# A GEGLU feed-forward kernel: the order of the first loads and of the first matmuls

## The chip, the cores and the metric

The kernel runs on one core of a Trainium2 chip. Its time is the device time in microseconds (us); three runs of the kernel before gave 299.04, 299.29 and 299.55 us, so the median is 299.29 us. A further execution was taken with the profiler; all rows below come from it.

The engines are named as in the profile: PE is TensorE's matmul, PEld its weight load, DVE is VectorE, ACT is ScalarE, POOL is GpSimd and SP is SyncE, which only issues transfers here. "ps" is PSUM, where PE writes; it has eight banks.

## The reference

With x of 1024 tokens (32 x 32) by 1024, and weights 1024 x 3584, 1024 x 3584 and 3584 x 1024, all bfloat16:

```python
def reference(x, w_gate, w_up, w_down):
    return (_gelu(x @ w_gate) * (x @ w_up)) @ w_down
```

`_gelu` is the tanh approximation.

## The kernel before, in words

**Tiles.** A matmul here contracts over 128 rows. The model dimension of 1024 is cut into DK = 8 pieces, numbered dk; a weight piece is `big[w][:, dk, slot]`, 128 x 128, and x must lie transposed in `xT[:, dk, token]`. The 3584 hidden columns are FM = 28 chunks of 128. A "unit" (an entry of `parts`, and the p in the schedule) is one chunk with a range of tokens. Units 0 to 7 are chunks 0 to 7 with tokens 0 to 255 (XA); units 8 to 15 are the same chunks with tokens 256 to 511 (XB); the other units have 512 tokens. A unit has a gate sum ("G") and an up sum ("U") in PSUM; units 0 to 7 keep both in one bank, the bank of their own number. In the text, "gate step dk of unit p" is the matmul that adds piece dk to the gate sum of unit p.

**Transposing x.** The first 256 tokens come as two blocks of 128 tokens, `xa[:, 0]` and `xa[:, 1]`. PE turns pieces dk 0 to 4 of each block by a matmul against an identity (`turn_xa`, L349 to L360, ten turns of 128 columns), and ACT copies the turned pieces from PSUM to `xT` in four groups, `XA_PS` (L131), whose entries are (bank, first dk, last dk + 1, first block, last block + 1). DVE turns pieces dk 5 to 7 of both blocks (L457 to L466, 16 instructions, the mark "XD") and begins only when both blocks have landed. The other tokens come later and are turned by DVE (L476).

**The order of PE's work** is the list `steps`, written out by hand (L170 to L188). Ahead of it stand ten matmuls on constants that write nothing that is used (`WARM`, L395 and L399). Then, in this order: the turns of dk 0 to 2 of block 0 and of block 1, the turns of dk 3 and 4 of block 0 and of block 1; then step dk = 0 of units 0 to 7, G and U; then dk = 1 to 5 of these units with G and U by turns, and so on. Each step on units 0 to 7 waits for the pieces of `xT` that it reads, for its weight piece, and for the copy of a turned group that lay in its bank (L369 to L379). PE works strictly in the order of the list.

**The order of the loads.** SP issues block 0 of x, then the weight pieces dk = 0 to 7, gate and up by turns, 256 KB each (L293, `load_w0`); ACT issues block 1 of x on its own queue (L297). Both then wait for the up piece of dk = 5 to land, and issue the rest of x (L288). SP and POOL load the later weights when PE has finished with the buffers.

**After that** units 8 and up are worked one by one: ACT makes the gelu of a finished gate sum (L445), DVE multiplies it by the up sum (L485) into `hT`; at the end the down projection (L423) is summed over the 28 chunks, and ACT and DVE copy its results out.

## Time and profile before

| | |
|---|---|
| median of three runs | 299.29 us |
| profiled execution: time, and span of the core | 298.9 us, 297.6 us |
| PE busy | 293.7 us, 99% of the span |
| DVE, ACT, POOL busy | 64.3, 42.4, 7.9 us |
| first matmul on constants | 0.77 us |
| first turn (L355) | 3.93 us |
| first gate step (L386) | 5.01 us |
| DVE's 16 turns for XD | from 4.23 us, for 8.69 us |

A row of the timeline gives start, duration, engine, line, operation, tiles written and read, and "xN" for N instructions merged; in square brackets stands the idle time before, and what ended it. The table by stretch gives for each engine its busy time and the number of instructions that began. Matmuls are pipelined: one of 512 columns is shown as 379 ns long, but the next one follows 219 ns after it (49 in 10.74 us, on the chain). So a rate is read from the starts, not from the durations. Some records of matmuls are missing from the trace, at even distances.

### The profile page before, as it was taken

How to read it: one execution, taken by the hardware profiler on the slowest of the kernel's cores; microseconds unless marked ns; L12 is line 12 of the kernel's file. 1: busy time of each engine (PE TensorE's matmuls, PEld its weight loads, DVE VectorE, ACT ScalarE, POOL GpSimd, SP SyncE). 2: the span in 40 equal slices, each digit the busy share in tenths (PEclk: the TensorE clock that was granted, in tenths of full speed). 3: DMA queues.
4: the chain of work that ended last, by engine and by line, in shares of the span. 5: the costliest groups of instructions: out<-in, count | busy, mean ns of one | idle time of the engine just before them, and what ended most of it. 6: DMA issues, size and time to landing. Idle time of an engine off the chain costs nothing.

```text
span 297.6 us, 3492 instructions
## 1 busy us (share of the span) xinstructions
PE 293.7 (99%) x1528; PEld 148.3 (50%) x1552; DVE 64.3 (22%) x108; ACT 42.4 (14%) x79; POOL 7.9 (3%) x14
## 2 busy tenths in 40 slices
PE   8999999999999999999999999999999999999997
PEld 6899644444444444444444444444444444444445
DVE  4669721111221111122111122110000000000000
ACT  4032211211111121111121111110000000000000
POOL 1001001020000002001000000000000000000000
PEclk9999999999999999999999999999999999999999
DMA  7988004766009301943104000000000100010001
GB/s 260 389 199 266 19 2 149 274 204 222 0 0 303 122 0 40 373 153 99 45 0 141 0 2 0 0 0 20 18 18 18 37 18 18 20 35 18 18 20 35
DMA packets 17806, 26.43 MB, mean 89 GB/s; under 512 B 1152, under 2 KB 11392, under 8 KB 17792
## 3 DMA queue, kind: packets, MB, share of 16 engines
q1 hardware_dynamic: 13840, 16.78, 17.1%
q0 software_dynamic: 2176, 8.39, 7.9%
q10 hardware_dynamic: 1776, 1.05, 1.4%
q8 instruction: 12, 0.20, 0.3%
q14 instruction: 2, 0.02, 0.0%
HBM read 24.12 MB, written 2.10 MB: 88 GB/s over the span
## 4 chain that ended last, share of the span: by engine, by line
PE 99%; issue 0%; ACT 0%
PE ps L386 65%; PE ps L423 32%; PE ps L400 1%; PE ps L355 0%; ACT xT L451 0%
## 5 line engine op out<-in xcount | busy, mean ns | idle before, releaser
L423 PE MATMUL ps<-wd,hT 128*128 128x512 bf16 (+2 forms) x468 | 96.5, 366 | 0.4
L386 PE MATMUL ps<-xT,wubig 128*128 128x512 bf16 (+2 forms) x395 | 79.6, 336 | 0.3
L386 PE MATMUL ps<-xT,wgbig 128*128 128x512 bf16 (+2 forms) x394 | 79.3, 336 | 0.3
L423 PEld LDWEIGHTS ps<-wd,hT 128*128 128x128 bf16 x476 | 45.5, 98 | 51.6
L485 DVE TENSOR_TENSOR hT<-tb,ps 128x512 bf16<-128x512 f32 (+1 forms) x64 | 38.8, 611 | 136.2 <-PE ps L386 136.2
L445 ACT ACTIVATE tb<-ps 128x512 f32<-128x512 f32 (+1 forms) x64 | 34.3, 544 | 157.7 <-PE ps L386 157.5
L386 PEld LDWEIGHTS ps<-xT,wgbig 128*128 128x128 bf16 x400 | 38.2, 98 | 31.4 <-DVE xT L476 0.3
L386 PEld LDWEIGHTS ps<-xT,wubig 128*128 128x128 bf16 x400 | 38.2, 98 | 31.4
L386 PE MATMUL ps<-xT,wgsmall 128*128 128x512 bf16 x126 | 30.1, 379 | 0.1
L386 PE MATMUL ps<-xT,wusmall 128*128 128x512 bf16 x125 | 29.8, 379 | 0.2
L491 DVE CAST xT<-ps 128x512 bf16<-128x512 f32 (+1 forms) x8 | 5.4, 675 | 89.6 <-PE ps L423 89.6
L386 PEld LDWEIGHTS ps<-xT,wgsmall 128*128 128x128 bf16 x128 | 12.5, 98 | 15.1
L386 PEld LDWEIGHTS ps<-xT,wusmall 128*128 128x128 bf16 x128 | 12.5, 98 | 15.1
L451 ACT ACTIVATE xT<-ps 128x512 bf16<-128x512 f32 (+1 forms) x9 | 5.1, 561 | 93.1 <-PE ps L423 93.1
L476 DVE STREAM_TRANSPOSE xT<-hT 128x128 bf16<-128x128 bf16 (+2 forms) x20 | 13.4, 696 | 0.0
L461 DVE STREAM_TRANSPOSE xT<-hT 32x192 bf16<-32x192 bf16 x16 | 8.2, 514 | 4.7 <-DMA hT<-in_x_dram 4.2
L282 POOL DMA_DIRECT2D wubig<-in_w_up_dram x3 | 2.7, 884 | 63.1 <-PE ps L386 63.1
L400 PE MATMUL ps<-const-bfloat16-1.0 128*128 128x512 bf16 (+1 forms) x10 | 3.1, 498 | 0.8 <-PEq L528 0.8
L282 POOL DMA_DIRECT2D wusmall<-in_w_up_dram x2 | 2.0, 993 | 47.1 <-PE ps L386 26.0
L276 POOL DMA_DIRECT2D wd<-in_w_down_dram x3 | 2.3, 766 | 19.1 <-PE ps L386 19.1
L400 PEld LDWEIGHTS ps<-const-bfloat16-1.0 128*128 128x128 bf16 x10 | 1.2, 139 | 2.4 <-issue 2.4
L438 ACT ACTIVATE xT<-ps 128x128 bf16<-128x128 f32 (+1 forms) x4 | 1.6, 436 | 2.1 <-PE ps L355 2.0
(10 smaller groups left out, 4.9 us busy)
## 6 DMA issues: line engine op xcount, KB each, us to landing
wd<-in_w_down_dram SPq DMA_DIRECT2D x4, 1024.0 KB, 11.5
wgbig<-in_w_gate_dram SPq DMA_DIRECT2D x3, 1024.0 KB, 5.8
wubig<-in_w_up_dram POOLq DMA_DIRECT2D x3, 1024.0 KB, 9.7
wd<-in_w_down_dram POOLq DMA_DIRECT2D x3, 1024.0 KB, 11.3
wgbig<-in_w_gate_dram SPq DMA_DIRECT2D x8, 256.0 KB, 5.8
wubig<-in_w_up_dram SPq DMA_DIRECT2D x8, 256.0 KB, 5.9
wgsmall<-in_w_gate_dram SPq DMA_DIRECT2D x2, 1024.0 KB, 5.8
wusmall<-in_w_up_dram POOLq DMA_DIRECT2D x2, 1024.0 KB, 9.7
```

Of the source, the lines that this page charges most:

```text
L276: ew.do(lambda: eng.dma_start(wd[:, a:b, :], wd_r[:, a:b, :]), clock=clock)
L282: ctx.set((w, j), ew.do(lambda: eng.dma_start(wbuf(w, buf)[:, :, 0:gsz * P], w_r[w][:, :, c0 * P:(c0 + gsz) * P]), clock=q))
L386: v = pe.do(lambda: eng.matmul(ps[:, bank, f0:f1], wbuf(w, buf)[:, dk, slot * P:(slot + 1) * P], xT[:, dk, t0:t1], start=first, stop=last ...
L400: pe.do(lambda: eng.matmul(ps[:, 0, 0:n], ones_w, ones_x[:, 0:n], start=True, stop=True), mark=False)
L423: v = pe.do(lambda: eng.matmul(ps[:, b, 0:ncols], hT[:, m, tc * P:(tc + 1) * P], wd[:, m, col0:col0 + ncols], start=(m == 0), stop=(m == F ...
L438: ctx.set(("XA", j), act.do(lambda: eng.activation(xT[:, k0:k1, P * b0:P * b1], ps[:, bank, 0:nt * (k1 - k0)].rearrange("p (k t) -> p k t" ...
L445: ctx.set(("A", i), act.do(lambda: eng.activation(t_bufs[i % NTB][:, 0:t1 - t0], ps[:, gb, g0:g1], ACTF.Gelu_apprx_tanh)))
L451: ctx.set(("E", ji), act.do(lambda: eng.activation(osb[:, tc, col0:col0 + ncols], ps[:, b, 0:ncols], ACTF.Copy)))
L461: v = dve.do(lambda: eng.transpose(xT[32 * a:32 * (a + 1), XA_DVE[0]:XA_DVE[1], XA[0]:XA[1]].rearrange("p k (b t) -> p k b t", t=P)[:, :, ...
L476: v = dve.do(lambda: eng.transpose(xT[:, dk, q[0]:q[1]].rearrange("p (c i) -> p c i", i=32), src))
L485: ctx.set(("D", i), dve.do(lambda: eng.tensor_tensor(hT[:, m, t0:t1], t_bufs[i % NTB][:, 0:t1 - t0], ps[:, ub, u0:u1], ALU.mult)))
L491: ctx.set(("E", ji), dve.do(lambda: eng.tensor_copy(osb[:, tc, col0:col0 + ncols], ps[:, b, 0:ncols])))
```

## The change

Five edits that belong together:

- SP issues block 0 of x, then the gate piece of dk = 0, then block 1 of x, and then the other weight pieces in their old order. ACT issues no block.
- The ten turns go block by block: dk 0 to 4 of block 0, then dk 0 to 4 of block 1.
- After the turns of each block, five units (0, 1, 2, 6 and 3) do gate step 0 on the 128 tokens of this block alone. So these five steps become ten, of 128 columns instead of 256. The other steps with dk = 0 follow in a slightly different order.
- The four groups that ACT copies are cut by block: dk 0 of block 0, dk 1 to 4 of block 0, dk 0 of block 1, dk 1 to 4 of block 1. A step waits for a group only if it reads its tokens or uses its bank.
- `WARM` has one matmul of 128 columns at its end instead of four.

```diff
-    XA_PS = [(3, 0, 1, 0, 1), (7, 0, 1, 1, 2), (4, 1, 3, 0, 2), (5, 3, 5, 0, 2)]
+    XA_PS = [(3, 0, 1, 0, 1), (4, 1, 5, 0, 1), (5, 0, 1, 1, 2), (7, 1, 5, 1, 2)]
...
-    for k0, k1 in ((0, 3), (3, XA_DVE[0])):
-        for b in range(2):
-            steps += [("X", b, dk) for dk in range(k0, k1)]
-    for key, ps_ in (("G", (0, 1, 2, 6, 3, 7, 4)), ("U", (0, 1, 2, 3)), ("G", (5,)), ("U", (7, 6, 4, 5))):
+    FIRST = (0, 1, 2, 6, 3)
+    for b in range(2):
+        steps += [("X", b, dk) for dk in range(XA_DVE[0])]
+        steps += [(p, "G", 0, (P * b, P * b + P)) for p in FIRST]
+    for key, ps_ in (("G", (4, 5)), ("U", (0, 1, 2, 3)), ("G", (7,)), ("U", (6, 4, 5, 7))):
         steps += [(p, key, 0, None) for p in ps_]
...
+        def load_xa(ew, eng, b):
+            ctx.set(("xa", b), ew.do(lambda: eng.dma_start(
+                xa[:, b, :], xa_r[:, b, :]), clock=Q_XA[b]))
+
         def early_loads(ew, eng, side):
-            ctx.set(("xa", side), ew.do(lambda: eng.dma_start(
-                xa[:, side, :], xa_r[:, side, :]), clock=Q_XA[side]))
+            if side == 0:
+                load_xa(ew, eng, 0)
+                load_w0(ew, eng, "wg", 0)
+                load_xa(ew, eng, 1)
             yield
             if side == 0:
                 for k in range(DK):
                     for w in ("wg", "wu"):
-                        load_w0(ew, eng, w, k)
+                        if (w, k) != ("wg", 0):
+                            load_w0(ew, eng, w, k)
...
-            for jx, (xbank, k0, k1, _b0, _b1) in enumerate(XA_PS):
-                if t0 == XA[0] and (xbank == bank or k0 <= dk < k1):
+            lead = i < NBIG
+            for jx, (xbank, k0, k1, b0, b1) in enumerate(XA_PS):
+                if lead and (xbank == bank or (k0 <= dk < k1 and P * b0 < t1 and t0 < P * b1)):
                     pe.wait(C_ACT, ctx.get(("XA", jx)))
-            if t0 == XA[0] and dk >= XA_DVE[0]:
+            if lead and dk >= XA_DVE[0]:
                 pe.wait(C_DVE, ctx.get("XD"))
...
-        WARM = [512] * 6 + [128] * 4
+        WARM = [512] * 6 + [128]
```

## The prediction

> **What bounds the kernel now.** I read the chain that ended last first, since it says whether a saving at the start can reach the end at all. Its pieces are start, duration, what:

> ```profile
> PE 293.7 (99%) x1528; PEld 148.3 (50%) x1552; DVE 64.3 (22%) x108; ACT 42.4 (14%) x79; POOL 7.9 (3%) x14
> ```
> ```profile
> 0.77 3.14 PE ps L400 x10
> 3.93 1.26 PE ps L355 x10
> 5.19 28.03 PE ps L386 x288
> 33.22 0.05 issue
> 33.27 10.74 PE ps L386 x49
> ```

> PE works from 0.77 us to the end without a wait that shows; the pieces of 0.05 us "issue" recur every 10.79 us after 49 matmuls and are missing records. So whatever shifts PE's first step with dk = 1 shifts the end by as much, unless something else then binds. The whole case is the stretch up to there. The timeline of it:

> ```profile
> 0.73 0.38 SPq L297 DMA_DIRECT2D hT<-in_x_dram  x1
> 0.79 0.38 ACTq L297 DMA_DIRECT2D hT<-in_x_dram  x1
> ...
> 3.90 1.04 PEld L355 LDWEIGHTS ps<-ident,hT 128*128 128x128 bf16 x10 [0.26 <-issue]
> 3.93 1.26 PE L355 MATMUL ps<-ident,hT 128*128 128x128 bf16 x10
> ...
> 4.23 8.69 DVE L461 STREAM_TRANSPOSE xT<-hT 32x192 bf16<-32x192 bf16 x16 [4.23 <-DMA hT<-in_x_dram]
> 4.26 1.62 ACT L438 ACTIVATE xT<-ps 128x128 bf16<-128x128 f32 x4 [2.04 <-PE ps L355]
> ...
> 4.97 0.70 PEld L386 LDWEIGHTS ps<-xT,wgbig 128*128 128x128 bf16 x7
> 5.01 0.95 PE L386 MATMUL ps<-xT,wgbig 128*128 128x256 bf16 x7
> ...
> 6.78 1.04 PE L386 MATMUL ps<-xT,wgbig 128*128 128x256 bf16 x8
> ...
> 7.59 0.81 PEld L386 LDWEIGHTS ps<-xT,wubig 128*128 128x128 bf16 x8
> ```

> The turns begin at 3.93, the steps at 5.01, and the first step with dk = 1 at 6.78. Two rates lie in it. Until about 5 us PE runs at half speed: the last ten turns of 128 columns follow each other by (1.26 - 0.31) / 9 = 0.105 us, and the weight loads of the 512-column matmuls on constants start at 1.15, 1.57 and 2.00, 0.43 apart. Later 128 columns take 0.057 (four in 0.225 us at 19.89), 256 columns 0.109 (eight from 6.78 to 7.65), 512 columns 0.219. The column of the granted clock says 1.00 everywhere, so the starts have to be read.

> Then when the loads land. Block 0 of x lands 3.1 us after its issue (3.8), block 1 on ACT's queue 3.3 after (4.1), the gate piece dk 0 at 1.17 + 3.6 = 4.8, the up piece at 1.64 + 4.0 = 5.6, and those of dk 1 at 2.11 + 4.5 = 6.6 and 2.58 + 5.0 = 7.6. The stretch table (stretch, length, busy time of PE, PEld, DVE, ACT, POOL, granted clock, DMA share, GB/s):

> ```profile
> 1.00:2.00 1.00, 1.00 (x4) 0.29 (x2) 0.00 (x0) 1.00 (x1) 0.59 (x2) 1.00 0.17 51
> 2.00:3.00 1.00, 1.00 (x4) 0.44 (x3) 0.00 (x0) 0.21 (x2) 0.00 (x0) 1.00 0.96 264
> 3.00:4.00 1.00, 0.98 (x7) 0.46 (x6) 0.00 (x0) 0.00 (x0) 0.00 (x0) 1.00 1.04 387
> 4.00:5.00 1.00, 1.00 (x10) 0.96 (x11) 0.74 (x2) 0.69 (x3) 0.00 (x0) 1.00 1.14 397
> ```

> The 16 DMA engines are full from 2 us on. The issues stand 0.47 us apart and the landings 0.7 to 1.0, so bytes set the landings, not issues.

> **The loads, part by part.** A load's landing is when the bytes up to it have moved, and a lag. The two blocks are 524 KB; 51 + 264 = 315 KB had moved at 3.0, so 524 KB at 3.0 + 209/387 = 3.54, and the second had landed at 4.09: a lag of 0.55. In the new order, 262 KB (block 0 alone) have moved at 2.0 + 211/264 = 2.80, landing at 3.35; the gate piece comes at 3.54 + 0.55 = 4.09; block 1 is the third and comes at 4.0 + 84/397 + 0.55 = 4.76, where the gate piece was. So block 0 gains 0.45 us and the gate piece 0.7; block 1 loses 0.67. This is an estimate. Bounds: block 0 not sooner at all (3.8); or all sooner, so that loads do not bind. The up piece of dk 0 and the rest are issued one place, 0.47, later on SP's queue: nothing, since the bytes ahead of them stay the same. ACT's queue loses an issue of 0.38 us beside its 1.28 us table load; it then idles 2.04 us, so nothing.

> **PE, part by part.** Three matmuls on constants go: 3 x 0.107 = 0.32 us, so PE is free at 3.39 (3.28 + 0.107). It is worth something only if block 0 is there: from landing to first turn is 3.93 - 3.8 = 0.13.

> New on the path is the way from a block's first turn to the step that reads it. Today's row: the turn of dk 0 of block 1 is the fourth, at 3.93 + 3 x 0.105 = 4.25; ACT copies it from 4.58 for 0.28; the first step starts at 5.01. That is 0.76 us, and the other turns hide all but 0.03 of it. In the new order five turns of 0.107 = 0.53 stand between, so PE idles 0.76 - 0.53 = 0.23 us, and does so twice, once a block.

> The split steps: five of 128 columns at half speed cost 0.53, five at full speed 0.28, together 0.81 against 5 x 0.109 = 0.55. Then eleven steps of 256 columns, 1.20. Weight loads (98 ns, five more) lie beside the matmuls.

> The sum, if loads never bind: turns from 3.39, steps from 4.15 to 4.68, turns to 5.21, steps from 4.68 + 0.76 = 5.44 to 5.73, and 1.20 more: dk = 1 begins at 6.93 instead of 6.78, +0.15. By the bytes: turns from 3.35 + 0.13 = 3.48, steps from 4.24 to 4.77 (the gate piece is ready at 4.22), block 1 from 4.89, steps from 5.65 to 5.93, then 7.13, +0.35. With block 0 as late as now: turns from 3.93, steps from 4.69 to 5.2, block 1 from there, steps from 5.96 to 6.25, then 7.45, +0.67. I take +0.3, between the first two: the bytes are the nearest row, but the row of 264 GB/s holds the second queue's start too, which goes away.

> What else could bind: DVE starts its 16 turns when block 1 is there, 4.76 + 0.14 = 4.90 instead of 4.23, and is done 8.69 later, at 13.59 instead of 12.92. The first step with dk = 5 loads its weights at 13.65 now, and at 13.95 with the shift. So 0.36 us of cover remain; without it, DVE's lateness would be paid in full. ACT's larger copy (0.60, of dk 1 to 4 of block 0) ends near 4.8, before block 1's first turn needs ACT at 5.0. The pieces of dk 1 land at 6.6 and 7.6; the later PE asks for them from 7.1 and 7.95. So the cost of 0.3 stands, and beside the median of 299.29 gives 299.6. (The profiled execution took 298.9, its span 297.6 and 1.3 around it; it lies 0.39 under the median, and the shift is added to the median.) A change of under 0.2%, 0.6 us, cannot be told from none here.

> **Rival 1, slower: the half speed lasts longer.** Full speed came near 5.1 us, after 4.3 us of work with one idle of 0.22 (from 3.71 to 3.93). The new order has the idle of 0.23 at 3.92 and a second, equal one near 5.3, just where full speed began. If idles start the count anew, 4.3 us count from the first one's end (4.2) to 8.5, or from the last one's (5.6) to 9.9. From 5.6 on PE then does half the work it would: (8.5 - 5.6) / 2 = 1.45 or 2.15 us lost. With the smaller, 299.6 + 1.5 = 301.1. It decides if full speed comes after 6.3 or so. For it: the four times spread by 0.65 us, more than a fixed start would give, and what 1.3 us more of half speed would cost. Against it: the idle of 0.22 before did not prevent full speed.

> [...]

> **Rival 2, slower: block 0 lands no sooner.** Its first packets may simply be slow; only 51 GB/s show between 1 and 2 us, when block 0 is alone anyway. Then the trimmed matmuls on constants are replaced by waiting, and the sum is the third above: 299.29 + 0.67 = 299.96, 300.0. Against it: from 2.25 us or so the two blocks share full engines.

> **Rival 3, faster: late weights go away.** The up piece of dk 1 lands at 7.6 just as its first weight load starts (7.59). In other executions it may come later and stall PE; that could be the 0.39 of the median over the profiled one. Fewer queues at the start might bring all pieces sooner. That gives 299.29 - 0.39 + 0.15 = 299.05, and with full speed from 4.2 on (the first five steps then 0.25 shorter) 298.8; a little run-to-run luck makes it over 0.2%. Against it: DVE's chain, begun by block 1, allows no gain at all unless block 1 lands by 4.8.

> **How the numbers follow.** The sum as forecast (299.6, own range 299.2 to 299.9): 0.42. Rival 1 (301.1): 0.27. Rival 2 (300.0): 0.19. Rival 3 (298.8 to 299.05): 0.12, of which 0.08 over the bound. Faster 0.08, within 0.2% 0.42 + 0.04 = 0.46, slower 0.27 + 0.19 = 0.46. The range from 299.0 to 301.2 leaves out most of rival 3 and the upper part of rival 1, about 0.2.

> **What would show it.** First turn at 3.4 to 3.5 (rival 2: 3.9); two gaps of 0.2 us in PE's starts, behind the fifth and the tenth turn; DVE's turns from 4.6 to 4.9; the first dk = 1 step at 6.9 to 7.15; no wait at dk = 5. Starts of 256-column steps 0.21 apart after 6 us would show rival 1. The prediction is wrong if dk = 1 begins before 6.7, or if the steps are still at half speed at 7 us.

## The result, and the profile after

Over 17 runs each, the changed kernel takes 300.26 us in the median (299.45 to 301.81) and the kernel before 299.18 us (298.91 to 299.94). The ratio of the means is 1.0041, with a 95% interval from 1.0026 to 1.0057: slower by 0.41%, that is 1.1 us by the medians and 1.2 by the means. The time lies inside the range of the prediction (299.0 to 301.2), but beyond its likeliest case (299.6, no change that can be told).

The times of the changed kernel do not scatter around one value. Sorted:

```
before: 298.91 298.96 298.98 299.04 299.05 299.13 299.15 299.18 299.18 299.23 299.29 299.45 299.46 299.46 299.55 299.67 299.94
after:  299.45 299.48 299.67 299.88 299.90 299.94 300.06 300.12 300.26 300.28   300.68 301.00 301.38 301.39 301.60 301.76 301.81
```

Ten are 0.3 to 1.1 us over the old median, seven are 1.5 to 2.6 us over it. The profiled execution took 299.9 us, so it belongs to the ten. Its timeline (start, duration, engine, line, operation):

```profile
0.72 0.38 SPq L298 DMA_DIRECT2D hT<-in_x_dram  x1
...
1.17 0.42 SPq L294 DMA_DIRECT2D wgbig<-in_w_gate_dram  x1
...
1.63 0.42 SPq L298 DMA_DIRECT2D hT<-in_x_dram  x1
...
3.65 0.73 PE L363 MATMUL ps<-ident,hT 128*128 128x128 bf16 x5
...
4.53 0.71 PE L395 MATMUL ps<-xT,wgbig 128*128 128x128 bf16 x5 [0.16 <-DMA wgbig<-in_w_gate_dram]
...
5.17 0.75 PE L363 MATMUL ps<-ident,hT 128*128 128x128 bf16 x5
5.22 3.79 DVE L470 STREAM_TRANSPOSE xT<-hT 32x192 bf16<-32x192 bf16 x7 [5.22 <-DMA hT<-in_x_dram]
...
5.87 0.67 PE L395 MATMUL ps<-xT,wgbig 128*128 128x128 bf16 x7
...
7.41 1.04 PE L395 MATMUL ps<-xT,wgbig 128*128 128x256 bf16 x8
```

The turns of block 0 begin 0.28 us sooner than the first turn before (3.65 against 3.93), but block 1 is turned only from 5.17, and the first step with dk = 1 begins at 7.41 instead of 6.78: +0.63. The rest of the loss stands much later, among the waits of PE's weight loads:

```profile
6.42 0.33 PEld L395 LDWEIGHTS ps<-xT,wubig 128*128 128x128 bf16 x4 [0.16 <-DMA wubig<-in_w_up_dram]
...
17.71 0.10 PEld L395 LDWEIGHTS ps<-xT,wubig 128*128 128x128 bf16 x1 [0.49 <-DMA wubig<-in_w_up_dram]
```

The last up piece (dk = 7), issued at 9.38, landed 8.3 us later at 17.67. PE's starts have a hole there of 0.37 us beyond their usual distance. 0.63 + 0.37 = 1.00, and the two profiled executions differ by 299.9 - 298.9 = 1.0.

### The profile page after: what moved, and what is told of

It reads as the page before. It is cut to its first block, busy times and chain, and to the rows that moved or that the text cites. A ratio compares the mean times of both kernels' runs of the same rounds, so it can differ in the third digit from the quotient of the medians.

```text
span 298.6 us, 3520 instructions
## 1 busy us (share of the span) xinstructions
PE 295.6 (99%) x1554; PEld 147.9 (50%) x1554; DVE 64.4 (22%) x108; ACT 42.6 (14%) x79; POOL 7.9 (3%) x14
## 4 chain that ended last, share of the span: by engine, by line
PE 93%; DMA 3%; SPq 3%; issue 0%; ACT 0%
PE ps L395 61%; PE ps L432 32%; DMA wubig<-in_w_up_dram 3%; SPq L294 2%; SPq L298 0%; ACT xT L460 0%
## 5 line engine op out<-in xcount | busy, mean ns | idle before, releaser
L395 PE MATMUL ps<-xT,wgbig 128*128 128x512 bf16 (+2 forms) x405 | 80.4, 335 | 0.2 <-DMA wgbig<-in_w_gate_dram 0.2
```

The lines of the kernel that those rows point to most:

```text
L395: v = pe.do(lambda: eng.matmul(ps[:, bank, f0:f1], wbuf(w, buf)[:, dk, slot * P:(slot + 1) * P], xT[:, dk, t0:t1], start=first, stop=last ...
```

## The experiments

Three theories were told apart. A: idle time of PE in the first microseconds keeps it at half speed for longer in some executions. B: the new order of the loads brings data late. C: the way from a turn over ACT's copy to the step is now paid for twice. Each batch was timed beside its own runs of the kernel before, with medians of 299.31 us (e1 to e4), 299.40 (e5 to e8) and 299.43 (e9 to e12); what is said of "over before" goes against these. The three batches ran on three different chips. Each ratio is one of means, with its 95% interval.

**e1_short_const: the shorter run on constants alone**

```diff
 (the kernel before)
-        WARM = [512] * 6 + [128] * 4
+        WARM = [512] * 6 + [128]
```

> The kernel before, with one 128-column matmul on constants instead of four, nothing else changed. PE's idle ahead of block 0 grows from 0.22 to about 0.54 us; no load and no step moves. Theory A (idle time early on makes PE stay at half speed longer in some executions): the times spread over more than the 1 us of the kernel before, some executions come out above 300.0, the median rises by 0.3 us or more. Theory B (the loss is late loads) and theory C (the loss is the wait for ACT's copy, paid twice): median and spread as before, 299.2 within 0.15, none above 300.1.

Measured: 299.16 us (298.88 to 299.75, 12 runs), ratio 0.9994 (0.9984 to 1.0003). PE's starts show the longer idle, 0.60 us ahead of the first turn, and the steps from 5.06 at full speed (seven of 256 columns from 5.06 to 5.82, 0.109 each):

```profile
2.42 1.17 PE L400 MATMUL ps<-const-bfloat16-1.0 128*128 128x512 bf16 x3
3.98 1.14 PE L355 MATMUL ps<-ident,hT 128*128 128x128 bf16 x10 [0.39 <-DMA hT<-in_x_dram]
5.06 0.92 PE L386 MATMUL ps<-xT,wgbig 128*128 128x256 bf16 x7
```

So this part of the change costs nothing, and an idle of 0.6 us in that stretch did not hold full speed back. A, in the form "any more idle", fell here.

**e4_order_only and e3_loads_only: the two halves of the change**

e4 keeps the old loads (block 1 on ACT's queue) and has all the rest of the change; e3 is the kernel before with the new loads alone.

```diff
 (e4: the changed kernel)
-            if side == 0:
-                load_xa(ew, eng, 0)
-                load_w0(ew, eng, "wg", 0)
-                load_xa(ew, eng, 1)
+            ctx.set(("xa", side), ew.do(lambda: eng.dma_start(
+                xa[:, side, :], xa_r[:, side, :]), clock=Q_XA[side]))
...
-                        if (w, k) != ("wg", 0):
-                            load_w0(ew, eng, w, k)
+                        load_w0(ew, eng, w, k)
```
```diff
 (e3: the kernel before)
-            ctx.set(("xa", side), ew.do(lambda: eng.dma_start(
-                xa[:, side, :], xa_r[:, side, :]), clock=Q_XA[side]))
+            if side == 0:
+                load_xa(ew, eng, 0)
+                load_w0(ew, eng, "wg", 0)
+                load_xa(ew, eng, 1)
...
-                        load_w0(ew, eng, w, k)
+                        if (w, k) != ("wg", 0):
+                            load_w0(ew, eng, w, k)
```

> The changed kernel with the old loads (block 1 on ACT's queue, gate piece third). Turns, split steps, groups and the short run on constants as in the changed kernel. Block 0 lands at 3.8, so turns from 3.93; the gate piece at 4.8, so steps from 4.93. Theory C: dk = 1 begins 7.3 to 7.7, all weight pieces land as before, time about 299.9 to 300.1 with little spread. Theory B: under 299.5, the loads being the old ones. Theory A: the spread of the changed kernel, some above 301.

> The kernel before with the new order of loads alone (block 0, gate piece, block 1, all on SP). The turns of block 1 stand fourth in PE's list and wait for block 1 near 5.1, so about 1.2 us of idle. Theory B: dk = 1 begins near 7.7 (+1.0), all weight pieces land 0.4 us later than before, the up piece of dk 7 past 17 us again, time 300.2 to 300.6. Theory A adds executions with 1.5 us on top: up to 302. Theory C alone: under +0.5.

Measured: e4 300.86 us (299.32 to 301.58, 12 runs), ratio 1.0042 (1.0025 to 1.0059), with 7 of 12 over 300.6. e3 300.52 us (300.1 to 302.36, 7 runs), ratio 1.0057 (1.0034 to 1.0081). Each half is slower alone. e3's median is theory B's number, and three of its seven executions lie near 302, as A adds. Its profile is of one of these, 302.05 us. PE waits there for block 1 and then for the up piece of dk 0, and the granted clock is 0.50 from 7.42 to 10.83 us:

```profile
5.40 0.64 PE L362 MATMUL ps<-ident,hT 128*128 128x128 bf16 x7 [1.21 <-DMA hT<-in_x_dram]
...
7.30 0.96 PE L393 MATMUL ps<-xT,wubig 128*128 128x256 bf16 x4 [0.23 <-DMA wubig<-in_w_up_dram]
```

e4's spread is theory A's; both B (under 299.5) and C (299.9 to 300.1 with little spread) miss it. e4's profile is of an execution of 301.55 us:

```profile
2.85 0.74 PE L402 MATMUL ps<-const-bfloat16-1.0 128*128 128x512 bf16 x2
3.91 0.73 PE L356 MATMUL ps<-ident,hT 128*128 128x128 bf16 x5 [0.32 <-DMA hT<-in_x_dram]
5.00 0.72 PE L388 MATMUL ps<-xT,wgbig 128*128 128x128 bf16 x5 [0.36 <-DMA wgbig<-in_w_gate_dram]
5.51 0.74 PE L356 MATMUL ps<-ident,hT 128*128 128x128 bf16 x5
6.19 1.14 PE L388 MATMUL ps<-xT,wgbig 128*128 128x128 bf16 x7
7.12 1.06 PE L388 MATMUL ps<-xT,wubig 128*128 128x256 bf16 x4
7.98 0.42 PE L388 MATMUL ps<-xT,wgbig 128*128 128x256 bf16 x1
8.19 1.06 PE L388 MATMUL ps<-xT,wubig 128*128 128x256 bf16 x4
9.04 1.44 PE L388 MATMUL ps<-xT,wgbig 128*128 128x256 bf16 x8
```

Four 256-column steps take from 7.12 to 7.98, 0.21 each: half speed, until past 9 us. Ahead of it PE stood for 0.53 us (3.28 + 0.107 to 3.91), 0.57 (behind the fifth turn, to 5.00) and 0.15 (to 6.19): 1.25 us of idle in less than 3.

**e2_filled and e5_order_filled: the idles filled**

Both put 128-column matmuls on constants into the idles, and leave loads and useful steps alone: e2 in the changed kernel, e5 in e4. A step "W" is such a matmul, with its bank and, where that bank was being copied, the group to wait for.

```diff
 (e2: the changed kernel)
+        steps += [("W", 0, None)] * 3 if b == 0 else [("W", 4, 1)]
         steps += [(p, "G", 0, (P * b, P * b + P)) for p in FIRST]
+        if b == 0:
+            steps += [("W", 7, None)]
...
-        WARM = [512] * 6 + [128]
+        WARM = [512] * 6 + [128] * 3
...
```
```diff
 (e5: against e4)
+        steps += [("W", 0, None)] * 4 if b == 0 else [("W", 4, 1)]
...
-        WARM = [512] * 6 + [128]
+        WARM = [512] * 6 + [128] * 5
...
```

> The changed kernel with matmuls of 128 columns on constants put into PE's idles: two more ahead of block 0, three behind its turns, one behind its steps, one behind the turns of block 1. Loads and useful work as in the changed kernel. Theory A: the executions above 300.6 go away, the median falls from 300.3 to 299.7 to 299.9. Theories B and C: the idles are waits on loads and copies and stay as long, so median 300.2 to 300.3 and executions up to 301.8 as in the changed kernel.

> The new order of PE's work with the old loads (as e4), and matmuls of 128 columns on constants in the idles: four more ahead of block 0, four behind its turns, one behind the turns of block 1. No useful step moves. Theory A (a window of about 3.4 us with too much idle takes or withholds full speed): the executions above 300.6, 7 of 12 in e4, go away or fall to 1 in 10; median 299.7 to 300.0. Rival (those executions come from late weight pieces or from the wait for ACT's copy): 4 or more in 10 stay above 300.6, median 300.6 to 300.9.

Measured: e5 299.88 us (299.24 to 300.28, 12 runs), ratio 1.0012 (1.0002 to 1.0023): none of 12 over 300.6, against 7 of 12 in e4. That is theory A's number: of the 1.55 us that e4's median lay over before, about 1.1 go (0.9 by the means) when PE is merely kept busy. Its profile has three idles of 0.38, 0.35 and 0.23 us left there, and full speed from 3.43 us on (four 256-column steps from 6.32 to 6.76, 0.11 each), in spite of a wait of 0.87 us for the gate piece of dk 1 at 8.17:

```profile
4.35 0.39 PE L413 MATMUL ps<-const-bfloat16-1.0 128*128 128x128 bf16 x4
4.93 0.45 PE L389 MATMUL ps<-xT,wgbig 128*128 128x128 bf16 x5 [0.19 <-DMA wgbig<-in_w_gate_dram]
```

e2 gained little, and theory A's number is missed there: 300.14 us (299.91 to 302.25, 10 runs), ratio 1.0033 (1.0019 to 1.0047), 4 of 10 over 300.6. The profile of its 302.25 us says why, and shows the loss of full speed best of all. PE's timeline, then the table by stretch (stretch, length, busy time and count of PE, PEld, DVE, ACT, POOL, granted clock, DMA share, GB/s):

```profile
4.80 0.22 PE L422 MATMUL ps<-const-bfloat16-1.0 128*128 128x128 bf16 x1
6.35 0.53 PE L366 MATMUL ps<-ident,hT 128*128 128x128 bf16 x5 [1.32 <-DMA hT<-in_x_dram]
```
```profile
0.77:3.75 2.98, 2.98 (x11) 1.33 (x12) 0.00 (x0) 1.44 (x2) 0.76 (x2) 1.00 0.59 183
3.75:7.16 3.41, 1.81 (x24) 1.30 (x23) 0.73 (x2) 1.34 (x4) 0.00 (x0) 1.00 0.94 305
7.16:10.57 3.41, 3.41 (x20) 2.44 (x19) 3.22 (x7) 0.35 (x1) 0.00 (x0) 0.50 1.06 405
10.57:14.00 3.43, 3.43 (x34) 3.06 (x32) 3.21 (x7) 0.00 (x0) 0.00 (x0) 1.00 1.05 388
```

The 1.00 of the first row is not to be trusted: the turns of 128 columns start 0.107 us apart until 3.70, which is half speed. Full speed came at 3.75. Block 1 landed only at 6.3, one matmul on constants could not cover that, and PE was busy for 1.81 of the 3.41 us from 3.75 to 7.16. For the next 3.41 us the granted clock is 0.50, though PE is busy all the time; then it is 1.00 to the end. e3's record has the same steps at 4.00, 7.42 and 10.83. So in these two profiles the granted clock changed at borders 3.41 us apart, and half speed followed a stretch with long idles: up to 1.32 us in e2, up to 1.21 us in e3.

**e8_blockwise: block by block, without the split steps**

```diff
 (against e4)
         steps += [("X", b, dk) for dk in range(XA_DVE[0])]
-        steps += [(p, "G", 0, (P * b, P * b + P)) for p in FIRST]
-    for key, ps_ in (("G", (4, 5)), ("U", (0, 1, 2, 3)), ("G", (7,)), ("U", (6, 4, 5, 7))):
+    for key, ps_ in (("G", FIRST + (4, 5)), ("U", (0, 1, 2, 3)), ("G", (7,)), ("U", (6, 4, 5, 7))):
...
-        WARM = [512] * 6 + [128]
+        WARM = [512] * 6 + [128] * 4
```

> Old loads, four 128-column matmuls on constants, turns block by block and groups by block, but no split steps: all steps of dk 0 have 256 columns and come after the turns of both blocks. One idle is left, 0.76 - 0.53 = 0.23 us, behind the turns of block 1. Theory C: 299.3 to 299.6, that is 0.2 to 0.3 over before. Theory A: no executions above 300.6, since PE is busy for over 80% of every window. If instead turning block by block is what costs, 300 and more.

Measured: 299.55 us (299.2 to 301.2, 11 runs, one over 300.6), ratio 1.0002 (0.9988 to 1.0017). C has the right size at most: 0.15 over before, not told from nothing. A expected no execution above 300.6, and there is one, 301.2. Turning block by block does not cost that can be told; what e4 has on top is the split steps, with the waits ahead of and between them, and the shorter run on constants, which cost nothing by itself in e1. Those two were not tried apart in the new order.

**e7_one_queue and e10_one_queue_filled: the queue alone**

e7 is the kernel before with both blocks issued by SP (block 0, block 1, gate piece). e10 adds six matmuls of 128 columns on constants behind the turns.

```diff
 (e7: the kernel before)
-            ctx.set(("xa", side), ew.do(lambda: eng.dma_start(
-                xa[:, side, :], xa_r[:, side, :]), clock=Q_XA[side]))
+            if side == 0:
+                for b in range(2):
+                    ctx.set(("xa", b), ew.do(lambda: eng.dma_start(
+                        xa[:, b, :], xa_r[:, b, :]), clock=Q_XA[b]))
```
```diff
 (e10: against e7, behind the turns)
+    steps += [("W", 0, None)] * 6
...
```

> The kernel before with both blocks of x issued by SP, in the order block 0, block 1, gate piece, up piece; PE's order is the old one. If bytes alone set the landings (the prediction's step): block 0 lands near 3.4 instead of 3.8, block 1 and the weights as before, time 299.2 within 0.2. If one queue starts more slowly than two: the weight pieces of dk 1 and later land 0.3 to 0.5 later, and the time rises by 0.3 to 0.5.

> As e7 (the kernel before, both blocks and all weights on SP's queue), with six matmuls of 128 columns on constants behind the ten turns, 0.64 us at half speed, in the idle ahead of the gate piece. It parts the 1.1 us that e7 lost. Theory A has part of it: the idle is covered, the executions above 301 (4 of 12) go and the median falls to 299.8 to 300.1; what is left over 299.4 is the slower loading. If loads are all of it: median 300.5 as in e7.

Measured: e7 300.49 us (299.36 to 301.95, 12 runs), ratio 1.0043 (1.0026 to 1.006); e10 300.13 us (299.45 to 301.51, 12 runs), ratio 1.0025 (1.0012 to 1.0038). The blocks landed as early as by the bytes (3.4 and 4.0 us), but in e7's profile the gate piece behind them landed at 6.70, and PE waited for it:

```profile
3.70 1.23 PE L357 MATMUL ps<-ident,hT 128*128 128x128 bf16 x10
6.75 0.94 PE L388 MATMUL ps<-xT,wgbig 128*128 128x256 bf16 x7 [1.81 <-DMA wgbig<-in_w_gate_dram]
```

So with the old order of PE's work and the old order of loads, moving one 256 KB load to SP's queue cost 1.1 us (the weights behind it are issued 0.47 us later). Both of e7's expectations, 0 and 0.3 to 0.5, miss that. In e10 the median lies just above theory A's band and one execution, 301.51, is still over 301. The filler takes about a third of the cost back, though the two intervals overlap; that the 0.7 left is the waiting for data itself is argued, not shown.

The prediction's rule that bytes alone set the landings is refuted. By the packets in e7's trace, the 786 KB up to the gate piece had moved at 4.44 us. The trace also shows 16 signals for each of these loads, and PE's wait ended with the last of them: half of the gate piece's signals had come by 4.63, the last two at 6.06 and 6.70, and its first step began at 6.75. In the changed kernel's profile 15 signals of the last up piece had come by 16.63, the last came at 17.67, and the weight load that waited for it began at 17.71. In the kernel before all 16 for the gate piece came between 4.52 and 4.80.

**e9_act_block1: two queues, but the second one later**

```diff
 (the changed kernel)
                 load_w0(ew, eng, "wg", 0)
+            else:
                 load_xa(ew, eng, 1)
...
-            act.do(lambda: eng.activation(warm[:, 0:1], const0, ACTF.Gelu_apprx_tanh))
+            v = act.do(lambda: eng.activation(warm[:, 0:1], const0, ACTF.Gelu_apprx_tanh))
+            act.wait(C_ACT, v)
```

> The changed kernel, but block 1 is issued by ACT, behind its first activation (near 2.25 us), so that it still comes after block 0 and near the gate piece. PE's order and the matmuls on constants are those of the changed kernel. If it matters that two queues are at work at the start: 1.1 MB moved by 5 us instead of 1.0, the gate piece of dk 2 at about 8.2 instead of 8.65, the lower half of the times 0.3 to 0.5 under that of the changed kernel (its lowest is 299.45). If bytes alone set the landings: times as the changed kernel, median 300.3. Theory A in both cases: some executions above 300.6, since the idles stay.

Measured: 304.69 us (304.23 to 305.75, 4 runs), ratio 1.018 (1.016 to 1.0201): both expectations missed by far. Issued at 2.24 us behind SP's first weight pieces, block 1 landed at 8.25, and PE stood for it. Its steps then stay at half speed up to the first ones with dk = 1, at 11.85: 2.85 us from 9.00 on, where the profile of 299.9 us has 1.54 for the same steps (5.87 to 7.41):

```profile
4.46 0.71 PE L396 MATMUL ps<-xT,wgbig 128*128 128x128 bf16 x5 [0.19 <-DMA wgbig<-in_w_gate_dram]
8.30 0.76 PE L364 MATMUL ps<-ident,hT 128*128 128x128 bf16 x5 [3.12 <-DMA hT<-in_x_dram]
```

So a second queue at work did not make the loads quick by itself: 279 GB/s from 2 to 5 us. What the kernels with quick first loads (before, e1, e4, e5, e8: 334 to 358 GB/s) share is that both queues start in the first microsecond, with the two blocks ahead of any weights.

**e6_x_later: the rest of x issued one piece later**

```diff
 (the changed kernel)
-            ew.wait(Q_W0[("wu", 5)], ctx.get(("wu0", 5)))
+            ew.wait(Q_W0[("wu", 6)], ctx.get(("wu0", 6)))
```

> The changed kernel, but the rest of x is issued when the up piece of dk 6 has landed instead of that of dk 5, 1.3 us later. If the transfers of x delay the last weight pieces, the wait of 0.37 us before the up step of dk 7 goes and the lower half of the times falls by 0.2 to 0.4 (lowest 299.1 to 299.3 instead of 299.45). If x is then late for DVE's turns, PE waits after 19 us instead and the time is the same or longer. Theory A on its own: no change, median 300.3.

Measured: 301.3 us (299.82 to 303.31, 12 runs), ratio 1.0066 (1.0044 to 1.0088). The up piece of dk 7 landed 8.5 us after its issue at 9.19, again at 17.7, though x was issued from 15.21 on instead of 13.37: moving x's transfers back did not bring it sooner. Instead PE now waits for DVE near 20 us, as the other branch said:

```profile
20.20 0.34 PEld L395 LDWEIGHTS ps<-xT,wgbig 128*128 128x128 bf16 x2 [0.21 <-DVE xT L485]
```

That does not explain a median 1.9 us over before, against 1.1 for the changed kernel, with 10 of 12 over 300.6; in its profile block 1 was late before the edit can act (turns from 5.74). The two intervals overlap, and why so many executions fell there stays open.

**e11_after_look and e12_after_look2: the changed kernel twice more**

> The changed kernel once more, for a second profile of it. Theory A: if it takes over 300.6, starts of 256-column steps 0.21 apart are found for about 3.4 us after 5.5 us; if under 300.3, none after 6 us.

> The changed kernel a third time, for a third profile, with the same reading: over 300.6 with a stretch of half speed of about 3.4 us that ends past 8 us, or under 300.3 with none after 6 us.

Both were of the upper group: 301.5 and 301.78 us. PE's timeline of e12:

```profile
3.46 0.73 PE L363 MATMUL ps<-ident,hT 128*128 128x128 bf16 x5
4.22 0.69 PE L395 MATMUL ps<-xT,wgbig 128*128 128x128 bf16 x5
6.06 0.75 PE L363 MATMUL ps<-ident,hT 128*128 128x128 bf16 x5 [1.15 <-DMA hT<-in_x_dram]
6.75 1.14 PE L395 MATMUL ps<-xT,wgbig 128*128 128x128 bf16 x7
7.69 1.06 PE L395 MATMUL ps<-xT,wubig 128*128 128x256 bf16 x4
8.54 0.42 PE L395 MATMUL ps<-xT,wgbig 128*128 128x256 bf16 x1
8.76 1.06 PE L395 MATMUL ps<-xT,wubig 128*128 128x256 bf16 x4
9.61 1.08 PE L395 MATMUL ps<-xT,wgbig 128*128 128x256 bf16 x8
```

Block 1 comes at 6.0 instead of 5.1, PE idles for 1.36 us, and four 256-column steps take 0.85 us until past 9 us, as theory A expects: full speed comes at about 9.7 us (eight 256-column steps from 9.61 to 10.53, 0.115 each), in e11 at about 9.1. The first step with dk = 1 begins at 9.61 instead of 6.78: +2.83, and the time is 301.78 - 298.9 = +2.88. In e11 it is 9.40, +2.62, and +2.6. So in the upper group the whole loss is made before 10 us, and it has two parts: block 1 later by 0.9 than in the profile of 299.9 us, and the steps with dk = 0 behind it, which take 2.86 (6.75 to 9.61) instead of 1.54 (5.87 to 7.41).

## Why the prediction was right or wrong

**The path.** Right: what shifts the first step with dk = 1 shifts the end by as much. In all three profiles of the changed kernel the shift, with the one late wait, gives the time to 0.05 us.

**The landings: the step that failed.** "Bytes set the landings" put block 0 at 3.35, the gate piece at 4.09 and block 1 at 4.76. After their issues they took 2.8, 3.3 and 3.5 us in the first profile, 2.6, 3.2 and 4.4 in e11, 2.6, 2.9 and 4.4 in e12: block 0 at 3.3 to 3.5 as predicted, the gate piece at 4.1 to 4.5, but block 1 at 5.1, 6.1 and 6.0. The step has two terms, the moment at which the bytes up to a load have moved, and a lag of 0.55 us from there to the landing, read off a single load. Both were too small for the third load, and where block 1 was latest, the lag by more (moments in us, the measured ones from the packets and the landing signals of the traces):

| third load in order of issue | bytes moved | landed | lag |
|---|---|---|---|
| block 1, as predicted | 4.21 | 4.76 | 0.55 |
| gate piece, kernel before | 4.27 | 4.80 | 0.53 |
| block 1, changed kernel, 299.9 us | 4.47 | 5.12 | 0.65 |
| block 1, e11 | 4.77 | 6.08 | 1.31 |
| block 1, e12 | 4.67 | 6.01 | 1.34 |
| gate piece, e7 | 4.44 | 6.70 | 2.26 |

The bytes first. From 2 to 5 us the stretch table has, for the kernel before and for the changed one:

```profile
2.00:5.00 3.00, 2.98 (x18) 1.86 (x17) 0.74 (x2) 0.90 (x5) 0.00 (x0) 1.00 1.05 350
```
```profile
2.00:5.00 3.00, 2.78 (x15) 1.41 (x13) 0.00 (x0) 1.07 (x4) 0.00 (x0) 1.00 0.90 301
```

The last column is 350 against 301 GB/s. In all the profiles it is 334 to 358 where SP and ACT issue a block each at the start (before, e1, e4, e5, e8), and 274 to 322 where not (after, e2, e3, e6, e7, e9 to e12). Then the lag. In e12 half of block 1's signals had come by 4.87, and the last two only at 5.94 and 6.01. The third load's lag is 0.53 to 0.66 us in the five profiles with a block on each queue, and 0.62 to 2.28 in the nine others. The kernel before already showed that it is no constant: its first four weight pieces lag by 0.53, 0.69, 0.79 and 1.02.

"Nothing" for the pieces behind was wrong for the same reason: the up piece of dk 0 landed at 6.4 instead of 5.7, and the last one at 17.7 instead of 15.9, the wait of 0.37. What holds the last signals back was not found. e7 shows the effect with one queue and the old order, e9 that a second queue from 2.2 us on did not cure it, and e4 and e5 that two queues did not rule it out: there the gate piece of dk 1 landed at 7.70 and 8.13, with half of its signals by 6.11 and 6.01.

**Rival 2** (block 0 no sooner) did not happen. **DVE's cover** held: its turns ran from 5.22 to 13.93 in the first profile, and no wait stands at dk = 5. **The way over ACT's copy** was sized about right, 0.70 us from the turn at 5.17 to the step at 5.87, with an idle of 0.15 for 0.23. Of the +0.63 up to the first step with dk = 1, the sum by the bytes had 0.35; the other 0.28 is how much later than in that sum block 1 was turned (5.17 for 4.89).

**Rival 1** (half speed lasts longer) is what makes the upper group, together with the late block 1. It had a chance of 0.27 as the outcome; it came true in seven of 17 executions, and not in the median. Its effect was right: 301.1 predicted, 301.0 to 301.8 for six of the seven. Its cause was not. It laid the blame on the two idles of 0.23 us, and let the count begin anew behind an idle. e1 has 0.6 us of idle and loses nothing, e5 has 0.95 in one stretch and keeps full speed; e2 and e3 show fixed stretches of 3.41 us. What tells the two kinds apart in these profiles is, by an estimate, how much idle falls into one stretch. Worked out from the starts (0.107 us for 128 columns at half speed), with the 3.41 us of e2 and e3 as the length of a stretch, matmuls fill 75, 82 and 87% of the stretch that ends in full speed in the first profile of the changed kernel, in e1 and in e8. They fill 62, 51 and 63% of the stretch behind which half speed went on in e11, e12 and e4 (counted back from where full speed came, since these traces have no record of the clock). Where the stretches begin differs from execution to execution: full speed came at 3.43 us in e5, 3.75 in e2, 5.07 in the kernel before and 5.79 in the first profile of the changed kernel. So the same idle could count in one execution and be forgiven in another. In the changed kernel the idle is mostly the wait for block 1, the step above that failed. The two combine: in e12 a load that was 0.9 us later cost 0.9 us of waiting and, through the clock, 1.3 more.

**The forecast as a whole.** The likeliest case, 299.6, is only what the changed kernel does at its best: three of 17 executions are at 299.7 or below, and the profiled one of 299.9 has +1.00 where the sum had +0.3. It was wrong as the middle, since it took block 1's landing from a rate and a lag measured under another order of issue, and so missed both the waiting and how often rival 1 comes true. That the median still lies in the range is owed to the room left for rival 1. The nearest number that the prediction names, rival 2's 300.0, is near by luck, since block 0 did land sooner. Three of its signs missed as well: the first turn came at 3.65 for 3.4 to 3.5, DVE's turns at 5.22 for 4.6 to 4.9, and dk = 1 at 7.41 for 6.9 to 7.15. Half speed at 7 us, named there as a sign of being wrong, is found in e11 and e12.

## What to carry to other kernels

Where the path is a chain of loads in a full DMA stage, the landing of a load that is moved onto another queue is not read from the bytes of the old order and one lag; give it a range as wide as the spread of the neighbouring landings (here the third load's lag was 0.53 to 2.28 us), and ask who waits for it. Work placed between two loads to fill a wait makes PE depend on each landing in turn, while work done after both depends on the last alone. And an idle of PE in the first microseconds was paid for a second time in e2, as a clock of 0.50 for the following 3.41 us; matmuls on constants in the idles show quickly (e4 against e5, 300.86 against 299.88 us) whether that is so.
